# Finer first loads and the whole first batch of V turned on chip, in a chunked attention followed by a feed-forward block

## The chip, the cores and the metric

One core of a Trainium2 chip runs the whole kernel as one program. The metric is the device time of one execution in microseconds; the number compared is the median of several runs.

## The reference, cut to what matters

Batch 4, 8 heads, 768 tokens, head size 64, 8 memory tokens. Attention runs in chunks of 32 queries, each seeing the memory, 16 tokens to the left, its own 32 and 8 to the right; then each token's 512 numbers go through a normalisation and a two-layer block with 2048 hidden units.

```python
for c in range(nc):                       # chunks of 32 queries
    l_start, r_end = max(0, c_start - 16), min(S, c_end + 8)
    k_full = concat([mem_k, k[:, :, l_start:r_end]]); v_full = concat([mem_v, v[...]])
    a = softmax(scale * q_c @ k_full.T)
    out[:, :, c_start:c_end] = a @ v_full
x = out.transpose(0, 2, 1, 3).reshape(B, S, 512)
xn = (x - mean) / sqrt(var + 1e-6) * g_ln
return x + relu(xn @ w_ch1) @ w_ch2       # w_ch1 512x2048, w_ch2 2048x512
```

## The kernel before, in words

**Tiles and pairs.** The 3072 tokens are 24 tiles of 128; tile `t` belongs to batch `t // 6`. Two tiles are a pair `u`, and the feed-forward block works on pairs: `up(u, s)` (L398), eight steps of eight matmuls into `upb[s % 2]` with a ReLU on ACT or DVE, and `down(u, part)` (L415), eight parts of four matmuls into `dnb`; the last part of a tile adds the residual on DVE (L426) and stores the tile from SyncE (L429).

**Attention of a tile.** `qk_products` (L279), 32 small matmuls of Q against K; `below_max` (L298), maximum and subtraction on DVE; `weights` (L306), the exponential on ACT; `pt` (L313), P turned on TensorE and copied out half by DVE, half by ACT; `val_products` (L328), P times V into `two`; `tokens` (L339), division and mean on DVE; `shift` (L352), mean subtracted on GpSimd ("P") or ACT ("A"); `root` (L368), the standard deviation, on ACT and GpSimd; `turn_x` (L380), the tokens turned and scaled.

**Layout.** An octet is 8 consecutive tokens of one head, one row of 512 numbers. K and Q are loaded as octets (`load_octets`, L111), turned by 16 small transposes for each head pair `j` (`turn`, L222), and copied into `KT` (with the memory's columns between, `to_stream`, L237, two copies) or `QD` (`to_rows`, L246, one copy). V is wanted with tokens on partitions in 12 groups of 64 queries, with 40 tokens of overlap; it is loaded so by `load_v_group` (L118), from rows of 128 bytes, and the doubled rows are copied by SyncE (`v_shared`, L155, `v_mem`, L159). For batch 0 most of V is turned instead: octets into `VT` (which is `KT[1]`), then `v_turn(g, engine)` (L261) turns group `g` back and copies it into `V[0]`.

**Order of the work.** It is written out by hand: all engines run their instructions in the order of the source. TensorE's fillers, `warm(n)` (L444), multiply zeros into `upb[1]`. PSUM for the turns comes from a list of banks in rotation (`slot`, L86). Loads go out on the GpSimd queue; outputs and SBUF-to-SBUF copies on SyncE. From the third pair on a plan puts the attention of pair `u + 1` between the steps of `up(u)` and `down(u - 1)` (L653 to L715).

**The first 75 us** (L471 to L651). First loads: mem_k, 72 octets of K, 64 of Q, four V groups; then W1 in four parts, 72 octets of V, W2 in four, the rest of K (24 octets, two loads of 24 rows) and of Q. Tiles 0 and 1 use V groups 0 to 3, loaded directly; `v_twice` (L468) copies their doubled rows. Pair 0's `up` starts when tiles 0 and 1 are turned (L562). In between stand scores 2 and 3, V's turn and groups 4 to 11, tiles 2 and 3. Pair 1's `up` holds the rest of Q; pair 0's `down` holds the rest of K and tiles 4 and 5 (L611 to L639); half of pair 1's `down` is then issued with the turn of batch 1's K.

## Time and profile before

| what | number |
|---|---|
| median of 3 runs | 259.06 us (258.75 to 259.46) |
| the profiled execution | 258.69 us, its span 257.0 us |
| TensorE (PE) busy | 241.1 us, 94% of the span, 3411 matmuls |
| DVE, ACT, POOL busy | 131.9, 120.1, 97.5 us |
| L403 `up` and L419 `down` matmuls | 100.1 and 97.1 us |
| L447 fillers | 51 matmuls, 15.2 us |
| loads on the GpSimd queue | 14.68 MB in 41600 packets |

The span is what the profiler saw from the first to the last instruction; the rest of the execution's time lies around it. Times in the views are microseconds from the start of the span. A line of a timeline gives start, length, engine, source line, operation, what is written and read, a count, and in brackets the idle time before it and what ended it. PEld is TensorE's loading of weights, POOL is GpSimd, SPq the issuing of transfers by SyncE. The granted clock is the share of TensorE's clock that the chip lets through, in tenths in the page's slices.

### The profile page before, as it was taken

The numbers are of one execution on the slowest core, as the hardware profiler recorded it, in microseconds if no ns is written. First come the engines' busy times: TensorE is split into PE (matmuls) and PEld (weight loads), VectorE is DVE, ScalarE is ACT, GpSimd is POOL, SyncE is SP. The second block draws the span as 40 slices with busy tenths as digits, with TensorE's granted clock in tenths as the row PEclk, the third lists the DMA queues.
The fourth block names the chain that finished last, engine by engine and source line by source line (L and its number), as shares of the span: only waits on it lengthen the run. The fifth ranks groups of instructions, "written<-read, shape, count | busy, mean of one in ns | idle before, by whom it ended". The sixth has DMA issues, their size and how long they took to land.

```text
span 257.0 us, 7795 instructions
## 1 busy us (share of the span) xinstructions
PE 241.1 (94%) x3411; PEld 167.0 (65%) x3411; DVE 131.9 (51%) x296; ACT 120.1 (47%) x231; POOL 97.5 (38%) x171
## 2 busy tenths in 40 slices
PE   8697987997999899999999999999999999999993
PEld 3364675874577667667677767676677777777751
DVE  5557656345855656356555555554643564541121
ACT  1243466435565554654554455456464544543300
POOL 8397210372993286732402739512113022120000
PEclk9968999999999999999999999999999999999999
DMA  4999997099999997853398469805200111011112
GB/s 54 154 111 202 212 206 136 3 140 148 131 111 130 191 124 81 53 70 95 48 169 160 61 43 99 91 5 126 54 11 34 43 43 41 3 45 41 41 41 83
DMA packets 46462, 23.35 MB, mean 91 GB/s; under 512 B 33308, under 2 KB 42724, under 8 KB 46380
## 3 DMA queue, kind: packets, MB, share of 16 engines
q0 software_dynamic: 41600, 14.68, 50.0%
q1 hardware_dynamic: 4828, 8.18, 11.0%
q8 instruction: 26, 0.43, 0.7%
q14 instruction: 8, 0.07, 0.1%
HBM read 29.33 MB, written 6.29 MB: 139 GB/s over the span
## 4 chain that ended last, share of the span: by engine, by line
PE 76%; DMA 10%; DVE 5%; ACT 3%; POOL 2%; issue 1%; SPq 1%; DVEq 0%; ACTq 0%; POOLq 0%
PE upb L403 31%; PE dnb L419 31%; DMA raw<-in_q_dram 4%; PE two L332 3%; PE one L228 3%; DMA w1c<-in_moe_w_ch_dram 3%; DMA V<-memv 3%; PE one L290 2%; PE one L384 2%; PE one L317 1%; DVE KT L241 1%; ACT xn L359 1%; DVE xs L342 1%; ACT PTz L326 1%; POOL raw L113 1%
## 5 line engine op out<-in xcount | busy, mean ns | idle before, releaser
L403 PE MATMUL upb<-xT,w1c 128*128 128x256 f16 x768 | 100.1, 274 | 1.6 <-DVE xT L390 1.6
L419 PE MATMUL dnb<-w2c,rT 128*128 128x512 f16 x384 | 97.1, 380 | 0.0
L403 PEld LDWEIGHTS <-w1c 128*128 128x128 f16 x768 | 80.0, 115 | 10.2 <-issue 1.1
L411 ACT ACTIVATE rT<-upb 128x512 f16<-128x512 f32 x90 | 53.4, 593 | 60.4 <-PE upb L403 60.1
L419 PEld LDWEIGHTS <-rT 128*128 128x128 f16 x384 | 35.0, 98 | 26.7
L355 POOL TENSOR_SCALAR xn<-xs,nmean 128x512 f16<-128x512 f32 x18 | 12.4, 691 | 77.2 <-DVE nmean L348 44.3
L426 DVE SCALAR_TENSOR_TENSOR xs<-dnb,rstd,xs 128x512 f32<-128x512 f32 x24 | 18.0, 750 | 30.4 <-PE dnb L419 29.8
L307 ACT ACTIVATE P<-sub 128x512 f16<-128x512 f32 x24 | 15.2, 632 | 30.9 <-DVE sub L301 30.9
L390 DVE TENSOR_TENSOR xT<-one,g_col 128x512 f16<-128x512 f16 x22 | 15.2, 690 | 24.4 <-PE one L384 23.1
L228 PEld LDWEIGHTS <-raw 96*64 96x64 f16 (+2 forms) x640 | 14.6, 114 | 9.6 <-issue 6.0
L374 POOL TENSOR_SCALAR veps<-ssq 128x1 f32<-128x1 f32 x24 | 4.5, 189 | 40.2 <-ACT sq L370 39.9
L300 DVE TENSOR_REDUCE nmx<-one 128x8 f32<-128x512 f32 x22 | 15.1, 685 | 6.4 <-PE one L290 6.4
L370 ACT ACTIVATE sq<-xs,nmean 128x512 f16<-128x512 f32 x24 | 17.2, 717 | 0.3
L341 DVE RECIPROCAL rec<-two 128x8 f32<-128x8 f32 x24 | 5.0, 207 | 23.6 <-PE two L332 23.2
L342 DVE CUSTOM_DVE_ANT_1 xs<-two,rec 128x512 f32<-128x512 f32 x24 | 16.6, 691 | 0.8
L332 PEld LDWEIGHTS <-PTz 128*64 128x64 f16 x384 | 8.4, 110 | 12.3 <-issue 8.2
L447 PE MATMUL upb<-zeros 128*128 128x512 f16 x51 | 15.2, 437 | 1.3 <-DVE zeros L471 1.3
L332 PE MATMUL two<-V,PTz 128*64 128x65 f16 x384 | 11.0, 198 | 5.3 <-DVE V L469 1.7
L301 DVE TENSOR_TENSOR sub<-one,nmx 128x512 f32<-128x512 f32 x22 | 15.2, 691 | 0.8
L228 PE MATMUL one<-identity,raw 96*64 96x96 f16 (+2 forms) x432 | 13.4, 206 | 1.4 <-DMA raw<-in_q_dram 1.4
L378 POOL TENSOR_TENSOR rstd<-veps,mhalf 128x1 f32<-128x1 f32 x24 | 13.3, 554 | 2.0
L135 POOL DMA_DIRECT2D V<-in_v_dram x16 | 13.7, 856 | 0.4 <-issue 0.4
(107 smaller groups left out, 224.3 us busy)
## 6 DMA issues: line engine op xcount, KB each, us to landing
out_dram<-xs SPq DMA_DIRECT2D x24, 256.0 KB, 2.7
raw<-in_k_dram POOLq DMA_DIRECT2D x3, 768.0 KB, 8.6
raw<-in_q_dram POOLq DMA_DIRECT2D x3, 768.0 KB, 12.5
w1c<-in_moe_w_ch_dram POOLq DMA_DIRECT2D x4, 512.0 KB, 10.2
w2c<-in_moe_w_ch_dram POOLq DMA_DIRECT2D x4, 512.0 KB, 13.7
V<-in_v_dram POOLq DMA_DIRECT2D x16, 77.0 KB, 3.2
V<-in_v_dram POOLq DMA_DIRECT2D x15, 56.0 KB, 3.9
V<-memv SPq DMA_DIRECT2D x6, 120.0 KB
```

Of the source, the lines that this page charges most:

```text
L228: nc.tensor.matmul(out=pv[64 * par : 64 * par + 64, n * r : n * r + n], lhsT=src[lo : lo + n, heads + par, r, :], rhs=identity[lo : lo + n ...
L301: nc.vector.tensor_tensor(out=s.rearrange("p (c k) -> p c k", c=8), in0=scores, in1=free(m, 0, [[1, 8], [0, 64]]), op=ALU.subtract,)
L307: nc.scalar.activation(out=P[t % 3], in_=sub[t % 2], func=ACTF.Exp, scale=0.125)
L332: nc.tensor.matmul(out=two[64 * gg : 64 * gg + 64, 128 * h : 128 * h + 65], lhsT=PTz[t % 3][:, 4 * (h // 2) + 2 * gg + h % 2, :, :], rhs=V ...
L342: nc.vector.tensor_tensor_reduce(out=x.rearrange("p (h d) -> p h d", h=H), in0=free(two, 0, [[128, 8], [1, 64]]), in1=free(r, 0, [[1, 8], ...
L370: nc.scalar.activation(out=sq, in_=xs[t % 9], func=ACTF.Square, bias=nmean[t % 6], scale=1.0, accum_out=ssq[i],)
L390: nc.vector.tensor_tensor(out=xT[(t // 2) % 3][:, :, 128 * i : 128 * i + 128], in0=pv.rearrange("p (d c) -> p d c", d=4), in1=free(g_col, ...
L403: nc.tensor.matmul(out=p[:, 256 * hb : 256 * hb + 256], lhsT=free(w1c[hc // 4][:, dt, :], hc % 4, [[4, 128]]), rhs=xT[u % 3][:, dt, :], st ...
L411: nc.scalar.activation(out=o, in_=i, func=ACTF.Relu)
L419: nc.tensor.matmul(out=p, lhsT=rT[u % 2][:, hc, 128 * i : 128 * i + 128], rhs=w2c[hc // 4][:, hc % 4, :], start=(hc == 0), stop=(hc == 15),)
L426: nc.vector.scalar_tensor_tensor(out=x, in0=p, scalar=rstd[t % 9], in1=x, op0=ALU.mult, op1=ALU.add,)
L447: nc.tensor.matmul(out=upb[1], lhsT=zeros[:, 0:128], rhs=zeros, start=True, stop=True,)
```

## The change

- K, Q and V of batch 0 are first loaded as 64 octets each. The other 32 octets of each come as 128 rows (head pair by octet) in two loads, one for each head of the pair, into `rest[i]`.
- W1 comes in two loads of 1024 columns; W2's four follow at once. The order on the queue is K, Q, V, rest of K, half W1, rest of V, half W1, rest of Q, W2, mem_v.
- The direct loads of V groups 0 to 3, `v_twice` and the SyncE copy of mem_v for them go; V is turned for all twelve groups, the first four before pair 0's `up`. The turn of mem_v and V's first part stand between the scores of tiles 0 and 1 and their values.
- Fillers: 39 instead of 51.
- Scores 3 move into pair 0's `up`, as do the rest of K and `pt(2)`; tiles 4 and 5 are scored in pair 1's `up`. The loads of batch 1 are issued earlier. Pair 1's `down` is no longer begun before the third pair; all eight parts lie in the loop.
- `shift` of tiles 2 and 3 is on GpSimd instead of ACT.

```diff
-    def load_rest(dst, src, lo, n):
-        for hg in range(2):
+    def load_rest(i, src):
+        for par in range(2):
             nc.gpsimd.dma_start(
-                out=dst[32 * hg : 32 * hg + n, :, :, :],
-                in_=dram(src, 4 * hg * HS + 512 * lo, [[512, n], [HS, 4], [1, 512]]),
+                out=rest[i][:, par, :, :],
+                in_=dram(src, par * HS + 512 * 64, [[2 * HS, 4], [512, 32], [1, 512]]),
             )
...
-    load_octets(0, k, 0, 0, 72, 0)
+    load_octets(0, k, 0, 0, 64, 0)
     load_octets(1, q, 0, 0, 64, 0)
-    load_mem_rows(0, 1)
     make_identity(nc, identity)
-    for g in range(4):
-        load_v_group(0, g)
+    load_mem(memv0, mem_v, H)
+    load_octets(2, v, 0, 0, 64, 0)
...
+    load_rest(0, k)
+    load_w1(0)
+    load_rest(2, v)
+    load_w1(1)
+    load_rest(1, q)
+    for c in range(4):
+        load_w2(c)
+    load_mem_rows(0, B)
+    ready_v(1, nc.gpsimd)
...
-    warm(7)
+    warm(4)
     for j in range(4):
         turn_k_first(j, "VA"[j % 2])
     for j in range(4):
         turn_q_first(j, 0, "AV"[j % 2])
-    warm(2)
     s0 = qk_products(0)
     s1 = qk_products(1)
     below_max(0, s0)
...
     turn_q_first(3, 32, "A")
+    warm(1)
+    pt(0)
     weights(1)
+    mem_turn(memVT, memv0, H)
+    mem_cols(VT, memVT, False)
+    turn_v_first(0, "A")
+    turn_v_first(1, "V")
+    turn_v_first(2, "A")
+    turn_v_first(3, "V")
+    warm(1)
+    pt(1)
+    v_turn(0, "V")
+    v_turn(1, "A")
+    nc.vector.memset(V[0][96:128, NG - 1, :, :], 0.0)
+    warm(3)
+    val_products(0)
+    v_turn(2, "V")
+    v_turn(3, "A")
+    tokens(0)
+    shift(0, "A")
     warm(2)
+    val_products(1)
     s2 = qk_products(2)
+    warm(2)
+    tokens(1)
+    shift(1, "A")
+    warm(2)
+    turn_x(0)
+    turn_k_rest(0, "A")
+    warm(2)
+    turn_x(1)
+    warm(2)
+    up(0, 0)
     below_max(2, s2)
     weights(2)
+    turn_k_rest(1, "V")
+    up(0, 1)
+    turn_k_rest(2, "A")
+    turn_k_rest(3, "V")
+    up(0, 2)
+    v_turn(4, "V")
+    s3 = qk_products(3)
+    below_max(3, s3)
+    weights(3)
+    up(0, 3)
+    pt(2)
+    v_turn(5, "A")
+    turn_v_rest(0, "A")
+    turn_v_rest(1, "V")
+    val(2, "P")
...
+    up(1, 0)
     s4 = qk_products(4)
     below_max(4, s4)
     weights(4)
+    up(1, 1)
+    v_turn(9, "V")
+    up(1, 2)
     s5 = qk_products(5)
     below_max(5, s5)
     weights(5)
+    up(1, 3)
+    root(1)
+    v_turn(10, "V")
+    up(1, 4)
+    pt(4)
     root(2)
+    up(1, 5, "V")
+    v_turn(11, "A")
     root(3)
...
+    up(1, 6)
     pt(5)
     val(4, "A")
+    up(1, 7, "V")
+    banks["list"] = one + upb
+    down(0, 0)
...
-        d = 5 if u == 2 else 0
+        d = 4 if u == 2 else 0
...
-            elif u > 2:
+            else:
                 down(u - 1, step // 2)
-            elif step % 4 == 3:
-                down(u - 1, 4 + step // 4)
```

More of the change, by code (lines that the diff above doesn't have):

```diff
@@ L54 @@
     last = sb.tile([128, 1], FP16, name="last")
-    w1c = [sb.tile([128, 4, 512], FP16, name=f"w1c{i}") for i in range(4)]
+    w1c = [sb.tile([128, 4, 1024], FP16, name=f"w1c{i}") for i in range(2)]
     w2c = [sb.tile([128, 4, 512], FP16, name=f"w2c{i}") for i in range(4)]
@@ L60 @@
     QD = [sb.tile([128, 4, S], FP16, name=f"QD{i}") for i in range(2)]
-    krest = sb.tile([64, 4, 8, 64], FP16, name="krest")
-    qrest = sb.tile([64, 4, 8, 64], FP16, name="qrest")
+    rest = [sb.tile([128, 2, 8, 64], FP16, name=f"rest{i}") for i in range(3)]
     sub = [sb.tile([128, 512], FP32, name=f"sub{i}") for i in range(2)]
@@ L169, in load_w1 @@
         nc.gpsimd.dma_start(
-            out=w1c[c], in_=dram(moe_w_ch1, 512 * c, [[FF, 128], [128 * FF, 4], [1, 512]])
+            out=w1c[c], in_=dram(moe_w_ch1, 1024 * c, [[FF, 128], [128 * FF, 4], [1, 1024]])
         )
@@ L404, in up @@
                     out=p[:, 256 * hb : 256 * hb + 256],
-                    lhsT=free(w1c[hc // 4][:, dt, :], hc % 4, [[4, 128]]),
+                    lhsT=free(w1c[hc // 8][:, dt, :], 512 * (hc // 4 % 2) + hc % 4, [[4, 128]]),
                     rhs=xT[u % 3][:, dt, :],
@@ L451, in turn_k_first @@
     def turn_k_first(j, engine):
-        to_stream(KT[0], turn(raw[0], 2 * j, 0, 72), j, engine, 72, 0)
+        to_stream(KT[0], turn(raw[0], 2 * j, 0, 64), j, engine, 64, 0)
     def turn_k_rest(j, engine):
-        pv = turn(krest, 2 * (j % 2), 32 * (j // 2), 24)
-        to_stream(KT[0], pv, j, engine, 24, 72)
+        to_stream(KT[0], turn(rest[0], 0, 32 * j, 32), j, engine, 32, 64)
     def turn_q_first(j, lo, engine):
@@ L461, in turn_q_rest, with turn_v_first, turn_v_rest @@
     def turn_q_rest(j, engine):
-        pv = turn(qrest, 2 * (j % 2), 32 * (j // 2), 32)
-        to_rows(0, pv, j, engine, 32, 64)
-    def turn_v(j, engine):
-        to_stream(VT, turn(raw[2], 2 * j, 0, 72), j, engine, 72, 24)
-    def v_twice(g0, g1):
-        nc.vector.tensor_copy(out=V[0][32:64, g0:g1, :, :], in_=V[0][64:96, g0:g1, :, :])
+        to_rows(0, turn(rest[1], 0, 32 * j, 32), j, engine, 32, 64)
+    def turn_v_first(j, engine):
+        to_stream(VT, turn(raw[2], 2 * j, 0, 64), j, engine, 64, 0)
+    def turn_v_rest(j, engine):
+        to_stream(VT, turn(rest[2], 0, 32 * j, 32), j, engine, 32, 64)
     nc.vector.memset(zeros, 0.0)
@@ L484 @@
     )
-    nc.vector.memset(memv16[:, :, :, 64:VW], 1.0)
-    nc.vector.memset(V[0][:, 0:4, :, 64:VW], 1.0)
-    nc.vector.memset(V[0][0:16, 0, :, :], 0.0)
+    load_rest(0, k)
[7 more added lines that the diff above has]
+    ready_v(1, nc.gpsimd)
+    nc.vector.memset(VT[:, :, 0:16], 0.0)
+    nc.vector.memset(VT[:, :, KC - 8 : KC], 0.0)
     for i in range(3):
@@ L491 @@
     nc.vector.memset(mhalf, -0.5)
-    nc.vector.memset(VT[:, :, KC - 8 : KC], 0.0)
-    load_w1(0)
-    load_w1(1)
-    load_octets(2, v, 0, 24, 96, 0)
-    load_mem(memv0, mem_v, H)
-    load_w1(2)
-    load_w1(3)
-    load_w2(0)
-    load_w2(1)
-    ready_v(1, nc.gpsimd)
-    load_rest(krest, k, 72, 24)
-    load_rest(qrest, q, 64, 32)
-    load_w2(2)
-    load_w2(3)
-    load_mem_rows(1, B)
-    v_mem(0, (64,), 4)
+    nc.vector.memset(V[0][:, :, :, 64:VW], 1.0)
+    nc.vector.memset(V[0][0:16, 0, :, :], 0.0)
+    nc.vector.memset(memv16[:, :, :, 64:VW], 1.0)
     five = one + dnb + [upb[0]]
@@ L513 @@
     mem_cols(KT[0], memKT[:, 0:4, :], True)
-    nc.vector.memset(V[0][:, 4:NG, :, 64:VW], 1.0)
-    warm(7)
+    warm(4)
     for j in range(4):
@@ L529 @@
     turn_q_first(3, 32, "A")
+    warm(1)
+    pt(0)
     weights(1)
+    mem_turn(memVT, memv0, H)
[15 more added lines that the diff above has]
+    shift(0, "A")
     warm(2)
+    val_products(1)
     s2 = qk_products(2)
-    pt(0)
+    warm(2)
[6 more added lines that the diff above has]
+    turn_x(1)
+    four = one + dnb
+    banks["list"] = four
+    warm(2)
+    up(0, 0)
     below_max(2, s2)
     weights(2)
-    warm(4)
-    pt(1)
-    nc.vector.memset(V[0][96:128, NG - 1, :, :], 0.0)
+    turn_k_rest(1, "V")
[13 more added lines that the diff above has]
+    val(2, "P")
+    turn_v_rest(2, "A")
+    turn_v_rest(3, "V")
+    up(0, 4)
+    pt(3)
+    v_turn(6, "V")
+    v_turn(7, "A")
+    up(0, 5)
+    turn_x(2)
+    val(3, "P")
+    load_octets(0, k, 1, 0, 96, 0)
+    load_octets(1, q, 1, 0, 96, 0)
+    load_v_group(1, 0)
+    up(0, 6, "V")
+    turn_q_rest(0, "A")
+    turn_q_rest(1, "V")
     nc.vector.tensor_copy(
@@ L542 @@
     )
-    warm(6)
-    v_twice(0, 2)
-    val_products(0)
-    tokens(0)
-    shift(0, "A")
-    v_twice(2, 4)
-    warm(2)
-    pt(2)
-    val_products(1)
-    tokens(1)
-    shift(1, "A")
-    warm(2)
-    turn_x(0)
-    warm(4)
-    turn_x(1)
-    s3 = qk_products(3)
-    warm(2)
-    four = one + dnb
-    banks["list"] = four
-    up(0, 0)
-    below_max(3, s3)
-    up(0, 1)
-    weights(3)
-    mem_turn(memVT, memv0, H)
-    mem_cols(VT, memVT, False)
-    up(0, 2)
-    up(0, 3, "V")
-    turn_v(0, "A")
-    turn_v(1, "V")
-    turn_v(2, "A")
-    turn_v(3, "V")
-    pt(3)
-    up(0, 4)
-    v_turn(4, "V")
-    v_turn(5, "A")
-    val(2, "A")
-    up(0, 5)
-    v_turn(6, "V")
-    v_turn(7, "A")
-    up(0, 6)
-    val(3, "A")
-    turn_x(2)
-    up(0, 7, "V")
-    v_turn(8, "A")
-    turn_x(3)
-    root(0)
-    up(1, 0)
-    v_turn(9, "V")
-    up(1, 1, "V")
-    v_turn(10, "A")
-    up(1, 2)
-    root(1)
-    up(1, 3, "V")
-    v_turn(11, "V")
-    load_octets(0, k, 1, 0, 96, 0)
-    load_octets(1, q, 1, 0, 96, 0)
-    for g in range(3):
-        load_v_group(1, g)
-    up(1, 4)
-    up(1, 5, "V")
-    turn_q_rest(0, "A")
-    turn_q_rest(1, "V")
-    up(1, 6)
+    up(0, 7)
+    v_turn(8, "V")
+    turn_x(3)
     turn_q_rest(2, "A")
     turn_q_rest(3, "V")
-    up(1, 7, "V")
-    turn_k_rest(0, "A")
-    turn_k_rest(1, "V")
-    banks["list"] = one + upb
-    down(0, 0)
-    turn_k_rest(2, "A")
-    turn_k_rest(3, "V")
-    down(0, 1)
+    root(0)
+    load_v_group(1, 1)
+    up(1, 0)
     s4 = qk_products(4)
@@ L618 @@
     weights(4)
-    down(0, 2)
+    up(1, 1)
+    v_turn(9, "V")
+    up(1, 2)
     s5 = qk_products(5)
@@ L622 @@
     weights(5)
+    up(1, 3)
[3 more added lines that the diff above has]
+    pt(4)
     root(2)
+    up(1, 5, "V")
+    v_turn(11, "A")
     root(3)
-    for g in range(3, 8):
+    for g in range(2, 5):
         load_v_group(1, g)
-    down(0, 3)
-    down(0, 4)
-    pt(4)
-    down(0, 5)
+    up(1, 6)
     pt(5)
     val(4, "A")
+    up(1, 7, "V")
+    banks["list"] = one + upb
+    down(0, 0)
+    down(0, 1)
+    val(5, "A")
+    down(0, 2)
+    turn_x(4)
+    mem_cols(KT[1], memKT[:, 4:8, :], True)
+    down(0, 3)
+    root(4)
+    for g in range(5, 9):
+        load_v_group(1, g)
+    down(0, 4)
+    turn_x(5)
+    root(5)
+    for g in range(9, NG):
+        load_v_group(1, g)
+    down(0, 5)
+    turn_k(1, 0, "V")
     down(0, 6)
+    turn_k(1, 1, "A")
+    turn_k(1, 2, "V")
     down(0, 7)
-    val(5, "A")
-    root(4)
-    root(5)
-    for g in range(8, NG):
-        load_v_group(1, g)
-    mem_cols(KT[1], memKT[:, 4:8, :], True)
-    down(1, 0)
-    turn_k(1, 0, "V")
-    turn_x(4)
-    down(1, 1)
-    turn_k(1, 1, "A")
-    down(1, 2)
-    turn_k(1, 2, "V")
-    turn_x(5)
-    down(1, 3)
     turn_k(1, 3, "A")
```

## The prediction

> **What bounds the kernel now.** I read the summary page first, then the busy time by stage, the chain of waits, and the instruction timelines of each engine up to 100 us. The page's slices:

> ```profile
> PE   8697987997999899999999999999999999999993
> ...
> PEclk9968999999999999999999999999999999999999
> ```

> TensorE is the bound: it is busy in nearly every slice after the eighth, and each slice is 6.4 us. The busy time by stage (columns: stretch, its length, busy us of PE, PEld, DVE, ACT and POOL, granted clock, DMA share, GB/s) says how much of it is not work:

> ```profile
> 0.00:29.44 29.44, 23.28 (x439) 13.21 (x440) 17.69 (x47) 9.48 (x19) 19.83 (x36) 0.88 1.06 140
> 29.44:100.00 70.56, 64.89 (x1082) 47.04 (x1081) 40.09 (x92) 37.42 (x76) 33.77 (x58) 1.00 0.94 130
> 100.00:245.00 145.00, 145.00 (x1858) 103.34 (x1857) 71.83 (x156) 72.57 (x135) 43.91 (x78) 1.00 0.41 64
> ```

> From 100 us on PE never idles, and the change touches nothing that is issued there. So the end moves by two things only: when the first `up` of the first pair starts (29.44 us, call it T0), and how much PE idles between T0 and 100 us (70.56 - 64.89 = 5.67 us). All 51 filler matmuls of `warm` (L447) lie before T0, so taking twelve away saves nothing by itself. The waits behind the 5.67 us (who waited for whom, us, times, longest):

> ```profile
> PE upb L403 <- DVE xT L390: 1.6, 2, 0.8
> PE two L332 <- ACT PTz L326: 1.5, 2, 1.3
> PE two L332 <- ACT V L273: 1.1, 2, 0.9
> PE two L332 <- DMA V<-memv: 0.6, 1, 0.6
> ```

> What sets T0 is a chain, read from the PE timeline (start, length):

> ```profile
> 12.66 0.42 PE L228 MATMUL one<-identity,raw 32*64 32x32 f16 x16 [1.39 <-DMA raw<-in_q_dram]
> ...
> 14.38 0.87 PE L290 MATMUL one<-KT,QD 64*32 64x64 f16 x50
> ...
> 28.26 0.40 PE L384 MATMUL one<-identity,xn 128*128 128x128 f16 x4 [0.35 <-ACT xn L359]
> ```

> Q lands at 12.62; the first scores start 1.76 us later; then softmax, P turned, values, tokens, x turned, 15.06 us in all. The last view is the granted clock in stretches of 3.41 us, at whose edges it changed:

> ```profile
> 10.78:14.19 3.41, 2.02 (x98) 1.58 (x90) 2.03 (x6) 2.05 (x6) 1.38 (x4) 1.00 1.46 108
> 14.19:17.60 3.41, 3.00 (x125) 2.56 (x126) 2.53 (x5) 0.91 (x3) 3.29 (x8) 0.50 0.90 84
> 17.60:21.02 3.42, 3.42 (x54) 1.63 (x50) 1.25 (x3) 1.97 (x5) 3.42 (x5) 0.50 1.24 202
> 21.02:24.43 3.41, 2.66 (x30) 1.44 (x29) 2.48 (x8) 1.25 (x3) 3.24 (x6) 1.00 1.24 201
> ```

> The same stretches for L447 alone hold 0.41, 0.26, 2.33 and 2.22 us of filler. After the one with 0.41 the clock fell to half; 3.00 busy us of small turns and scores did not bring it back, 2.33 us of filler did; 1.66 and 1.78 us in two other stretches kept it.

> **Part 1: the loads.** The first K, 72 octets, is issued at 2.03 and lands at 10.00, Q at 12.62. After, both have 64 octets: 64 KB less before Q is complete. At the 162 GB/s of the stretch from 5 to 8 us that is 0.4 us: Q at 12.2. The other end comes from the later K and Q of batch 1 (96 rows each, 1536 KB, 196 GB/s from 54 to 57 us): issued at 50.85, the second landed at 62.76, 11.9 us; with the 2.7 us of the small mem_k load as the fixed part, (11.9 - 2.7) x 1024/1536 + 2.7 = 8.8, so Q at 10.9. The second is nearer in kind, a K and a Q back to back in the same queue, so I lean there: **11.2**.

> [...]

> The queue behind: POOL's loads wait for the landing of the one eight loads earlier (the first fetch of qrest waited 3.07 us for raw V, the load eight before it). In the new order none starves the queue: 2.9 MB lie ahead of the end of the first W1 half, at about 0.2 MB/us from 4 us on, so it lands near 20, the second half near 27, long before T0 and the fifth `up`. V's rest (near 22) and the 1.0-1.5 us memsets of `ready_v` (done near 26) are covered as well. The four direct V groups with their SyncE copies and `v_twice` go; with them the 0.97 and 0.75 us PE waits on L469.

> **Part 2: from the first scores to T0.** Times from the start of the first scores. P0 is ready at 3.6 (14.38 to 17.96, unchanged: ACT still copies Q first). Then `pt` of tile 0 (0.6 at half clock), DVE 0.42, ACT 0.58: 5.5. ACT now has exp 1 (0.63) and two V turns (0.70 for 72 octets, so 0.65 each): 7.45; DVE's two V turns, 0.75 each behind the mem copies (0.19 + 0.26), end at 7.65. Only then can `v_turn` 0 and 1 start: 8.7; ACT copies the second (0.57) behind P1's half (0.58): 9.3. `warm(3)` ends at 9.85 at half clock (0.43 each), value products 10.4, `v_turn` 2 and its DVE copy 11.15, which stands on DVE ahead of `tokens(0)`; that takes 0.21 + 0.69 + 0.08 + 0.15 and issue: 12.35. Value products 1, scores 2 and `warm(4)` in two calls follow, `tokens(1)` 13.95, the ACT shift 14.7, x turned twice with `turn_k_rest(0)` and two fillers between, DVE 0.69: T0 at **18.0** if the clock stays at half to the end. With PE's rows at their full-clock length (a filler 0.22, `pt` 0.39, a turn 0.30 against 0.47) from the first score on, the same list gives 13.3; with full-clock lengths only after 24.4 us, 16.0; only after 27.8 us, 17.1.

> Which? The new order has hardly a filler from 8.3 us to the first value products, so the drop at 14.19 stays. The stretch to 17.6 and the next hold one or two fillers (0.4 to 0.9 us), that to 24.4 `warm(3)` (1.3 us), that to 27.8 six (2.6 us). Only the last passes the 2.33 that was seen to suffice: clock back at 27.8, T0 = 11.2 + 1.76 + 17.1 = **30.1**, 0.7 us later than now. So V's turn, which adds about 4 us of ACT and DVE work in the chain, eats the earlier Q and the fillers that go.

> [...]

> **Part 3: from T0 to 100 us.** PE work: out go `mem_turn` of V (0.34), four turns of 72 octets (33.49 to 34.73: 1.24) and one K rest (0.30); in come scores 3 (0.34), `pt(2)` (0.24) and four turns of V's rest (two of Q's rest took 0.61, so 1.2): -0.1 us. No filler lies here. The waits, scheduled by hand on four engines with `up` 0.97 (PE), ReLU 0.60, exp 0.63, max and subtract 0.69 each, root 0.90, PTz 0.42 (DVE) and 0.58 (ACT):
> - pair 0: DVE does two softmaxes before `val(2)`; exp 3 cannot start until 6.0 after T0, and ReLU 3, ACT's half of PTz 2 and V 5 stand behind it on ACT: 8.45. PE is there at 6.85: **1.6** (now 1.16 + 0.23 in the same place). xT 3 before pair 1: **0.2** (now 0.50 + 0.78).
> - pair 1: exp 4 and 5 wait for DVE with ReLUs behind them, and roots 1 to 3 (2.7 us) come in the same ten microseconds: **0.2** on `upb`. Then `down(0, 0)` writes dnb0, where `pt(5)` was put; ACT's copy of it stands behind root 2, V 11, root 3 and a ReLU and ends at 29.9, PE is there at 28.5: **1.4** (now 1.30 at the value products).
> - pair 2: its `down` is now full, so V's mem rows (issued by SyncE after the outputs of `down(0, 7)`, about 8 us as now) have 11.8 us of PE work before value products 6: no wait where now 0.62; the rest (now 1.07) **0.4**, as a `down` lies between the last values and the turn.

> Sum 3.8 against 5.67, -1.9. The batch 1 loads start some 10 us earlier; V groups on POOL end later than root 5 by 11 us, but tile 6 needs only the first four. If that cover goes, the 0.62 comes back.

> **Sum.** The profiled execution took 258.69 (span 257.0 and 1.7 around it): 258.69 + 0.7 - 0.1 - 1.9 = 257.4. It lay 0.37 under the median of the runs, 259.06, so on that scale **257.8**.

> **Rivals.**
> - *The clock stays up.* For it: small matmuls are busy time too, and 0.97 us of filler before 10.78 may suffice. Against: 14.19 to 17.60. T0 = 13.0 + 13.3 = 26.3: -3.1 - 0.1 - 1.9, **253.9**.
> - *Slower: the clock is still at half when `up` begins.* Place: the stretch up to 27.8 with six fillers spread between waits. For it: a stretch just under 2.33. T0 31.2 with 0.2 for Q's turns at half, +1.8; one more stretch of 3.41 us of `up` at half loses 1.7: +1.8 + 1.7 - 0.1 - 1.9 = +1.5, **260.6**. It decides once T0 and the loss on the `up`s together pass 29.44 + 2.0 + 0.8 = 32.2.
> - *The waits only move.* ACT is 53% and DVE 57% busy now from T0 to 100 us, but by the list above ACT has 9.3 us of work in 11.3 us of pair 1; if each in-order wait costs a little more, 5.7 us idle stays: +0.7 - 0.1 = +0.6, **259.7**, no measurable change.

> **Chances.** Forecast 0.45 (256.6 to 259.0, which covers Q at 10.9 to 12.2 and the clock back at 24.4), clock up 0.20, clock down 0.20, waits move 0.15. A measurement of this kernel tells about 0.3% (0.8 us) from no change. Faster: 0.33 of the forecast's and 0.20: 0.53. Same: 0.10 and 0.10: 0.20. Slower: 0.02, 0.05, 0.20: 0.27. The range reaches to both outer rivals: 254.0 to 260.7.

> **What would show it.** Right: Q landing near 11.2; granted clock 0.50 from about 14 to 28; T0 near 30; a PE wait of 1 to 2 us on ACT before value products 2 and before `down(0, 0)`; no wait on V's mem rows; PE idle from T0 to 100 us near 3.8. Wrong: a clock back before 22 (time near 254), T0 past 32, a PE wait on W1 or V's rest, or idle time above 5.7 after T0.

## The result and the profile after

| | before | after |
|---|---|---|
| median of 4 runs each, same chip | 258.9 us (258.68 to 259.46) | 261.72 us (261.12 to 262.48) |
| ratio, 95% interval | | 1.0107 (1.007 to 1.0144) |
| the profiled execution, its span | 258.69, 257.0 us | 261.19, 259.5 us |
| Q's landing | 12.62 | 10.14 |
| first scores | 14.38 | 11.83 |
| T0, the first `up` of pair 0 | 29.44 | 32.88 |
| granted clock at half | 14.19 to 21.02 | 13.26 to 26.91 |
| PE idle in the 70.56 us after T0 | 5.67 | 4.41 |

The change costs 2.8 us, 1.1%, and the time lies outside the predicted range. The table says where: Q comes 2.5 us earlier, the waits after T0 shrink by 1.3, and yet T0 is 3.4 us later. Line numbers of the changed kernel are one lower than before's (L402 for L403); an experiment with a line added has its own.

The summary page of after: TensorE's busy share in slices of 6.5 us, the granted clock, and the queue that brings instructions (packets, MB, share).

```profile
PE   8948897998999989999999999999999999999992
...
PEclk9955999999999999999999999999999999999999
...
q8 instruction: 27, 0.44, 0.7%
```

The third slice (13.0 to 19.5 us) has fallen to 4 where before had 9. The busy time by stage shows that the rest of the kernel is as it was:

```profile
32.88:103.44 70.56, 66.15 (x1124) 48.35 (x1125) 41.54 (x96) 38.67 (x78) 35.34 (x59) 1.00 0.81 108
103.44:248.44 145.00, 145.00 (x1827) 102.97 (x1826) 70.76 (x152) 72.02 (x135) 42.24 (x75) 1.00 0.40 62
```

Idle after T0 is 70.56 - 66.15 = 4.41 us, and PE is still full in the last stretch. So the loss is ahead of T0. PE's timeline there:

```profile
11.83 1.09 PE L289 MATMUL one<-KT,QD 64*32 64x64 f16 x55
16.53 0.31 PE L289 MATMUL one<-KT,QD 64*32 64x64 f16 x9 [3.60 <-issue]
...
20.94 0.24 PE L227 MATMUL one<-identity,raw 64*64 64x64 f16 x2
22.45 1.01 PE L227 MATMUL one<-identity,raw 64*64 64x64 f16 x30 [1.28 <-issue]
...
32.88 1.04 PE L402 MATMUL upb<-xT,w1c 128*128 128x256 f16 x8 [0.44 <-DVE xT L389]
```

This is the finding. PE stops in the middle of a group of equal matmuls: after 55 of the 64 scores of tiles 0 and 1, and after 2 of the 16 matmuls that turn V's third head pair into one bank (the timeline merges them with those of the fourth). Their inputs are there: K and Q of both tiles come from the same turns and copies as those of the scores that ran, and V is one load into one tile. The profile names no semaphore and writes "issue". Number PE's recorded instructions from 0, matmuls, weight loads and the two of other kinds at the start together: the first stop is before number 449 and the second before number 705, 256 later. Before has the first at the same number, though another program leads up to it; its T0 is the second line:

```profile
15.66 0.39 PE L290 MATMUL one<-KT,QD 64*32 64x64 f16 x14 [0.41 <-issue]
...
29.44 1.91 PE L403 MATMUL upb<-xT,w1c 128*128 128x256 f16 x16
```

| block from | PE enters the block before | packet starts to ends | the last instruction started in the block before ends | PE enters |
|---|---|---|---|---|
| before, 449 | 10.88 | 13.28 to 14.17 | 15.26 | 15.66 |
| before, 705 | 15.66 | 19.44 to 20.34 | 22.05 | 22.10 |
| after, 449 | 10.41 | 13.75 to 15.11 | 12.82 | **16.53** |
| after, 705 | 16.53 | 20.12 to 21.17 | 21.09 | **22.45** |

In these four rows the packet starts 2.4 to 3.8 us after PE has entered the block before, takes 0.9 to 1.4 us, and when PE is waiting its code runs 1.3 to 1.5 us after the packet's end (first, third and fourth row; 1.4 to 1.5 at 449 in the three experiments below whose packet times are given). In after PE needed only 2.4 us (10.41 to 12.82) for a block of small matmuls. The transfers of 10 to 24 us (busy share of the DMA engines in 40 slices; packets by queue):

```profile
DMA  9999999999999999999999999999999999999999
...
q0 software_dynamic: 3411, 2.75, 117.5%
q8 instruction: 2, 0.03, 1.1%
```

Two instruction packets stand among 3411 data packets, with the DMA engines busy 90% or more in every slice. The two stops cost PE 3.60 + 1.28 = 4.88 us. (These waits count from the end of the last matmul, 12.92 and 21.18, a little later than the ends in the table.)

### The profile page after: what moved, and what is told of

Same layout as the page of the kernel before. It is cut to its first block, busy times and chain, and to the rows that moved or that the text cites. A ratio compares the mean times of both kernels' runs of the same rounds, so it can differ in the third digit from the quotient of the medians.

```text
span 259.5 us, 7955 instructions
## 1 busy us (share of the span) xinstructions
PE 242.7 (94%) x3495; PEld 169.5 (65%) x3495; DVE 131.2 (51%) x298; ACT 121.7 (47%) x237; POOL 93.5 (36%) x164
## 4 chain that ended last, share of the span: by engine, by line
PE 90%; DVE 3%; issue 3%; ACT 2%; DVEq 0%; ACTq 0%
PE upb L402 33%; PE dnb L418 33%; PE one L227 5%; PE upb L446 5%; PE two L331 3%; PE one L289 3%; PE one L383 2%; PE one L316 2%; PE dnb L227 1%; PE upb L227 1%; DVE xT L389 1%; PE one L267 1%; ACT rT L410 1%; DVE sub L300 1%; DVE nmx L299 1%
## 5 line engine op out<-in xcount | busy, mean ns | idle before, releaser
L402 PE MATMUL upb<-xT,w1c 128*128 128x256 f16 x768 | 100.9, 274 | 2.1 <-DVE xT L389 1.9
L402 PEld LDWEIGHTS <-w1c 128*128 128x128 f16 x768 | 79.6, 115 | 10.9 <-issue 1.6
L410 ACT ACTIVATE rT<-upb 128x512 f16<-128x512 f32 x93 | 55.1, 593 | 59.9 <-PE upb L402 59.7
L418 PEld LDWEIGHTS <-rT 128*128 128x128 f16 x384 | 35.3, 98 | 27.8 <-issue 1.3
L354 POOL TENSOR_SCALAR xn<-xs,nmean 128x512 f16<-128x512 f32 x20 | 13.9, 695 | 97.7 <-DVE nmean L347 50.3
L227 PEld LDWEIGHTS <-raw 96*64 96x64 f16 (+2 forms) x640 | 15.3, 118 | 8.2 <-issue 8.0
L299 DVE TENSOR_REDUCE nmx<-one 128x8 f32<-128x512 f32 x21 | 14.4, 687 | 9.8 <-PE one L289 9.8
L227 PE MATMUL one<-identity,raw 96*64 96x96 f16 (+2 forms) x432 | 14.0, 209 | 1.3 <-issue 1.3
L289 PEld LDWEIGHTS <-QD 64*32 64x32 f16 x768 | 7.3, 93 | 11.9 <-issue 11.3
L300 DVE TENSOR_TENSOR sub<-one,nmx 128x512 f32<-128x512 f32 x21 | 14.5, 691 | 0.7
L446 PE MATMUL upb<-zeros 128*128 128x512 f16 x39 | 13.6, 490 | 1.3 <-DVE zeros L468 1.3
L240 DVE COPY KT<-one 128x192 f16<-128x192 f16 (+4 forms) x24 | 10.9, 495 | 6.5 <-PE one L227 5.0
L377 POOL TENSOR_TENSOR rstd<-veps,mhalf 128x1 f32<-128x1 f32 x24 | 13.3, 556 | 2.0
## 6 DMA issues: line engine op xcount, KB each, us to landing
w2c<-in_moe_w_ch_dram POOLq DMA_DIRECT2D x4, 512.0 KB, 16.8
```

The costliest lines, as they stand in the source:

```text
L227: nc.tensor.matmul(out=pv[64 * par : 64 * par + 64, n * r : n * r + n], lhsT=src[lo : lo + n, heads + par, r, :], rhs=identity[lo : lo + n ...
L299: nc.vector.tensor_reduce(out=m, in_=scores, axis=AX.X, op=ALU.max)
L300: nc.vector.tensor_tensor(out=s.rearrange("p (c k) -> p c k", c=8), in0=scores, in1=free(m, 0, [[1, 8], [0, 64]]), op=ALU.subtract,)
L402: nc.tensor.matmul(out=p[:, 256 * hb : 256 * hb + 256], lhsT=free(w1c[hc // 8][:, dt, :], 512 * (hc // 4 % 2) + hc % 4, [[4, 128]]), rhs=x ...
L410: nc.scalar.activation(out=o, in_=i, func=ACTF.Relu)
L418: nc.tensor.matmul(out=p, lhsT=rT[u % 2][:, hc, 128 * i : 128 * i + 128], rhs=w2c[hc // 4][:, hc % 4, :], start=(hc == 0), stop=(hc == 15),)
```

## The theories

- **A, the code.** PE's next 256 instructions wait behind the data loads that the new order puts on the queue early (V, the rests, W1), and PE has less work between the two edges to cover it. Hold the loads back and the wait goes; the place is tied to the instruction's number.
- **B, the chain.** V's turn, now in front of the first values, and the engines it occupies make T0 late; "issue" is a label for something that belongs to these instructions.
- **C, the fillers.** Twelve fillers fewer leave the clock at half for longer, and that is the time lost.

## The experiments

All times are against before on the same chip, whose median was 259.03 to 259.06 in the three groups. "Gaps", or code waits, are the two waits at instructions 449 and 705.

### All later loads held back until Q is turned

```diff
-    load_mem(memv0, mem_v, H)
-    load_octets(2, v, 0, 0, 64, 0)
...
-    ready_v(1, nc.gpsimd)
...
         turn_q_first(j, 0, "AV"[j % 2])
+    nc.gpsimd.tensor_copy(out=gate, in_=QD[0][:, 3, 0:1])
+    load_mem(memv0, mem_v, H)
+    load_octets(2, v, 0, 0, 64, 0)
+    load_rest(0, k)
...
+    ready_v(1, nc.gpsimd)
```

The copy into `gate` makes GpSimd wait for Q's last turned columns before it issues the loads.

> The changed kernel, with every load after the first K and Q issued only when Q's first 32 octets have been turned. Theory A (code): PE stands still at its 449th and 705th instruction because the next 16 KB of its program is fetched only when it enters the 16 KB before, and that fetch waits behind the data loads. Then the first gap (3.60 us now) falls below 0.8, the second (1.28 now) becomes 1 to 3 as W1 is in flight, T0 comes to 29.5 to 31 and the time to 258.5 to 260. Theory B (chain): the gaps belong to the work there (a bank, a copy) and T0 is late through V's turn and the half clock. Then the gaps stay, V lands 4 us later, T0 is 33 or later, time 261.5 or more.

Measured: 259.82 us (257.92 to 261.43, 10 runs), ratio 1.0033 (0.9996 to 1.007); T0 30.40. PE's waits from 10 to 33 us:

```profile
PE dnb L228 <- DMA raw<-in_v_dram: 2.0, 1, 2.0
PE two L332 <- DVE xsum L342: 0.7, 1, 0.7
PE one L290 <- issue: 0.5, 1, 0.5
```

The 3.60 is 0.52 and the 1.28 is gone, with not one PE instruction changed. (For the second I had expected 1 to 3 us.) The packet for block 449 now runs from 11.42 to 12.38, against 13.75 to 15.11. A new wait of 1.95 us for V, which lands at 19.21 instead of 13.44, takes part of it back.

### V after Q's turn, everything else after V's turn

```diff
         turn_q_first(j, 0, "AV"[j % 2])
+    nc.gpsimd.tensor_copy(out=gate[:, 0:1], in_=QD[0][:, 3, 0:1])
+    load_mem(memv0, mem_v, H)
+    load_octets(2, v, 0, 0, 64, 0)
...
     turn_v_first(3, "V")
+    nc.gpsimd.tensor_copy(out=gate[:, 1:2], in_=VT[:, 3, 16:17])
+    load_rest(0, k)
...
+    ready_v(1, nc.gpsimd)
```

> As before it, but V's first part alone is issued after Q's turn, and everything after that (rests, W1, W2) only when V's first part has been turned, some 16 us after the start. Theory A: both gaps fall below 0.8 us, T0 comes to 28 to 29.5, time 257 to 258.5. Theory B: the gaps stay, T0 33 or later, time 261.5 or more.

Measured: 267.29 us (266.79 to 267.98), ratio 1.0318 (1.0291 to 1.0345). The gaps are 0.72 and none, as A has it, but the kernel is far slower:

```profile
34.90 1.47 PE L403 MATMUL upb<-xT,w1c 128*128 128x256 f16 x6 [4.16 <-DMA w1c<-in_moe_w_ch_dram]
```

W1 lands at 34.86, PE stands for it, and the clock falls to half twice more (34.5 to 41.35 and 48.2 to 51.6). The gain that I expected is missed: holding loads back has a price as soon as one of them is needed at T0.

### 120 more PE instructions of no more work

```diff
-        for _ in range(n):
+        w = 512 // parts
+        for _ in range(n * parts):
             nc.tensor.matmul(
-                out=upb[1], lhsT=zeros[:, 0:128], rhs=zeros, start=True, stop=True,
+                out=upb[1][:, 0:w], lhsT=zeros[:, 0:128], rhs=zeros[:, 0:w], start=True, stop=True,
             )
...
-    warm(20)
+    warm(20, 4)
```

> The changed kernel with each of the first 20 fillers cut into four of 128 columns: the same PE time before the first K, 120 more PE instructions. Theory A: the gaps stay at the same instruction numbers, so they move 120 instructions forward in the program, the first to before the first scores, with about 2 us each; T0 is 1 to 2.5 us earlier, time 259 to 260.7. Theory B: the gap stays inside the scores of tile 1 with 3.6 us; T0 and time (261 to 262.5) unchanged.

Measured: 261.67 us (260.88 to 262.36), ratio 1.0098 (1.0069 to 1.0127).

```profile
13.95 0.29 PE L227 MATMUL upb<-identity,raw 32*64 32x32 f16 x5 [2.01 <-issue]
...
20.43 0.29 PE L227 MATMUL one<-identity,raw 32*64 32x32 f16 x5 [3.08 <-issue]
```

Both stops have left the scores and V's turn and stand in turns of Q, which are other instructions and again numbers 449 and 705. So the place belongs to the count; B's reading of "issue" falls. A's price is missed: 5.09 us instead of 4.88, T0 33.30 instead of 32.88, no gain. Moving the blocks' edges did not help here.

### Before, with its first K as 64 octets and 8

```diff
-    load_octets(0, k, 0, 0, 72, 0)
+    load_octets(0, k, 0, 0, 64, 0)
+    load_octets(0, k, 0, 64, 72, 64)
```

> The kernel before with one edit: the first K as 64 octets and, right behind, the other 8 in a small load of their own. Both theories: K and Q land earlier, Q near 10.5 instead of 12.6. Theory A: the program's block at instruction 449 is not there before about 15, so T0 is at most 0.7 us earlier, time 258.2 to 259. Theory B: the chain simply starts 2 us earlier, T0 27.5, time 256.5 to 257.2.

Measured: 257.36 us (257.1 to 257.51), ratio 0.9932 (0.9912 to 0.9951). Q lands at 11.25 instead of 12.62, T0 is 28.08 instead of 29.44, and the clock is at half only from 16.30 to 19.71. The wait at 449 grows as A says, but A's time, 258.2 to 259, is missed: I had the code there at about 15, and its packet ran from 12.02 to 13.13 (13.28 to 14.17 in before), so PE went on at 14.6. Why it started 1.2 us after PE entered the block before, and not 2.4 as in before, was not tried. The wait costs less than Q brings:

```profile
14.61 0.29 PE L290 MATMUL one<-KT,QD 64*32 64x64 f16 x14 [1.06 <-issue]
```

### V issued when K is turned, the rest when Q is turned

```diff
         turn_k_first(j, "VA"[j % 2])
+    nc.gpsimd.tensor_copy(out=gate[:, 0:1], in_=KT[0][:, 0, 16:17])
+    load_mem(memv0, mem_v, H)
+    load_octets(2, v, 0, 0, 64, 0)
     for j in range(4):
         turn_q_first(j, 0, "AV"[j % 2])
+    nc.gpsimd.tensor_copy(out=gate[:, 1:2], in_=QD[0][:, 3, 0:1])
+    load_rest(0, k)
...
+    ready_v(1, nc.gpsimd)
```

The loads' old places are empty, as above.

> The changed kernel, V's first part issued when the first of K's turns is copied (about 10.4 us, just after PE enters the block whose start sends for the code at 449), all other loads when Q has been turned. Theory A (code): the fetch for 449 finds the queue nearly empty, so that gap is below 0.8 us; V lands near 16, so the 1.95 us that PE waited for V in the version with everything held back goes too; the fetch for 705 is behind V and the rests and costs 0 to 1.5. T0 28 to 29.5, profiled time 256.5 to 258. Theory B (chain and clock): V or the gap costs the same as in the version held back, T0 30 to 31, 258.5 to 260.

Measured: 257.37 us (255.85 to 258.62, 9 runs), ratio 0.9929 (0.9903 to 0.9955); T0 29.04.

```profile
11.78 1.09 PE L290 MATMUL one<-KT,QD 64*32 64x64 f16 x55
13.53 0.31 PE L290 MATMUL one<-KT,QD 64*32 64x64 f16 x9 [0.66 <-issue]
...
18.36 1.01 PE L228 MATMUL one<-identity,raw 64*64 64x64 f16 x30 [0.17 <-issue]
...
29.04 1.04 PE L403 MATMUL upb<-xT,w1c 128*128 128x256 f16 x8 [0.44 <-DVE xT L390]
```

The gaps fall from 4.88 to 0.83 us, V (16.71) is in time, and T0 comes 3.84 us earlier: the change's own PE program, with the loads in another order, is 0.7% faster than before instead of 1.1% slower. Packet 449 starts 0.5 us after PE has entered the block before (10.36, then 10.85 to 12.07), not 3.3.

### After, with the twelve fillers back

```diff
-    warm(4)
+    warm(7)
...
+    warm(2)
     s0 = qk_products(0)
...
-    warm(1)
+    warm(3)
     pt(0)
...
-    warm(1)
+    warm(3)
     pt(1)
...
-    warm(3)
+    warm(6)
     val_products(0)
```

> The changed kernel with twelve fillers put back before the first values (51 in all): 7 before K's turn, 2 before the first scores, 3 and 3 before the two turns of P, 6 before the first values. Theory A: the gaps at 449 and 705 stay, the fillers only add; T0 32.5 to 34, time 261 to 262.8. Rival C (the fillers that went are the cost, by the half clock): the clock is back one or two stretches of 3.41 us earlier, T0 31 to 32, time 259.5 to 260.8.

Measured: 263.26 us (262.83 to 264.78), ratio 1.0169 (1.0121 to 1.0216); T0 34.80, gaps 3.53 and 0.50, clock at half from 14.96 to 28.61: four stretches of 3.41 us, as in after. T0 and time lie above even A's ranges, and far from C's. The fillers cost time and raise no clock earlier. C falls.

### `pt(5)` in another PSUM bank

```diff
+    banks["turn"] += 2
     pt(5)
+    banks["turn"] -= 2
```

> The changed kernel with the turn of P of tile 5 in another PSUM bank, so that the first part of pair 0's down need not wait for it. All theories: the wait of 1.08 us before that part goes and nothing takes its place, as the waits after T0 are apart from what happens before: 0.8 to 1.1 us less than the changed kernel, 260.6 to 261.0.

Measured: 260.2 us (258.9 to 261.04, 10 runs), ratio 1.0035 (1.001 to 1.006). In after PE's waits from 32 to 105 us hold

```profile
PE two L331 <- ACT PTz L325: 1.3, 1, 1.3
PE dnb L418 <- ACT PTz L325: 1.1, 1, 1.1
```

and here the second line is gone; idle after T0 goes from 4.41 to 3.34. T0 is also 0.83 us earlier, with gaps of 3.12 and 1.27, although nothing ahead of it was touched; so the 1.5 us between the medians of the two versions, more than the 0.8 to 1.1 expected, are not the bank's alone.

### Both edits together

V issued when K is turned, the rest when Q is turned, and `pt(5)` in the other bank; of the two diffs:

```diff
+    nc.gpsimd.tensor_copy(out=gate[:, 0:1], in_=KT[0][:, 0, 16:17])
...
+    nc.gpsimd.tensor_copy(out=gate[:, 1:2], in_=QD[0][:, 3, 0:1])
...
+    banks["turn"] += 2
     pt(5)
+    banks["turn"] -= 2
```

> Both of these edits, the order of the loads and the bank. Theory A: the gains add, T0 28 to 29.5, profiled time 255.5 to 257. Theory B: 257.5 to 259.

Measured: 255.02 us (254.53 to 255.34), ratio 0.9834 (0.9805 to 0.9863). No wait at 449 or 705 is left, T0 is 27.91, idle after it 3.34; T0 and time are a little better than expected. This version beats both kernels, by 1.7% of before.

### Exponential 3 issued after tile 2's values

On top of both edits:

```diff
     below_max(3, s3)
-    weights(3)
...
     val(2, "P")
+    weights(3)
```

> The version with the loads held back and the other bank, and one edit more: the exponential of tile 3 on ACT is issued after the values of tile 2, so that the ReLU of pair 0's step 3, ACT's half of tile 2's P and group 5 of V no longer stand behind it. If the wait of 1.29 + 0.39 us before the values of tile 2 comes from that order on ACT, as the prediction put it, it falls to 0.6 to 1.0 and the time from 255.0 to 254.0 to 254.6. If it comes from DVE's half of P or from V's turn on PE, it stays and so does the time.

Measured: 255.22 us (254.47 to 257.98, 6 runs), ratio 0.9861 (0.9823 to 0.9898). The wait for ACT's half of PTz 2 shrinks as foreseen:

```profile
PE two L332 <- ACT PTz L326: 0.4, 1, 0.4
PE two L332 <- ACT V L273: 0.4, 1, 0.4
```

It was 1.3; idle after T0 is 2.45 instead of 3.34. So ACT's order caused it. The median is no better than that of the version before it: the 0.9 us do not show in runs that spread by 3.5.

### Before with the 64 octets and its loads held back

```diff
-    load_octets(0, k, 0, 0, 72, 0)
+    load_octets(0, k, 0, 0, 64, 0)
+    load_octets(0, k, 0, 64, 72, 64)
...
         turn_k_first(j, "VA"[j % 2])
+    nc.gpsimd.tensor_copy(out=gate[:, 0:1], in_=KT[0][:, 0, 16:17])
+    load_mem_rows(0, 1)
+    for g in range(4):
+        load_v_group(0, g)
...
         turn_q_first(j, 0, "AV"[j % 2])
+    nc.gpsimd.tensor_copy(out=gate[:, 1:2], in_=QD[0][:, 3, 0:1])
+    load_w1(0)
...
+    v_mem(0, (64,), 4)
```

> The kernel before with K as 64 and 8 octets, and its loads held back in the same way: mem_v and V groups 0 to 3 until K's first turn is copied, the rest until Q is turned. Theory A (code): the gap of 1.06 us at instruction 449 that the split of K alone left falls below 0.4; the small V packets come later, which may cost some of it at the first values. T0 27.2 to 28.2, time 256.3 to 257.4. If holding the loads back helps by something else than the code fetch, the gap stays.

Measured: 258.05 us (256.55 to 258.69, 11 runs), ratio 0.9954 (0.9933 to 0.9975). The code wait at 449 is gone, but the direct V groups now land at 13.6 to 18.1 and PE waits for their doubled rows:

```profile
21.65 0.44 PE L333 MATMUL two<-V,PTz 128*64 128x65 f16 x16 [1.32 <-DVE V L470]
24.29 0.44 PE L333 MATMUL two<-V,PTz 128*64 128x65 f16 x16 [1.44 <-DVE V L470]
```

They were 0.88 and 0.98 us without the hold. T0 is 27.90 against 28.08, and the median is 0.7 us above the one without the hold; I expected a gain. Its profiled execution is 0.16 us faster instead, so why the medians lie so far apart stays open.

## Why the prediction was wrong, point by point

**The step that failed** is Part 2, "T0 = 11.2 + 1.76 + 17.1 = 30.1". Its list has a duration for every instruction of four engines and takes for granted that PE's instructions are there. The 17.1 us from first scores to T0 became 21.05 (11.83 to 32.88), and 4.88 us of code wait lie inside. In the version with V issued early, where 0.83 us of it are left, the same distance is 29.04 - 11.78 = 17.26, and its 257.37 stands beside the forecast 257.8. That closeness is partly luck: the clock there came back at 23.39, not at 27.8. For a clock back at 24.4 the same list gave 16.0; with 0.83 of code wait that is 16.8, still within 0.5 us of the 17.26. In before the distance is 15.06, so what the forecast said of V's turn, that it eats the earlier Q, agrees with the runs once the code is there: this version and before with its K split end at the same 257.4.

The sum on the profiled executions, against the predicted 257.4 and the measured 261.19:

| term | predicted | measured | difference |
|---|---|---|---|
| start of the first scores (Q 11.2 + 1.76) | 12.96 | 11.83 | -1.13 |
| first scores to T0 | 17.1 | 21.05 | +3.95 |
| idle after T0 | 3.8 | 4.41 | +0.6 |
| other time after T0, against before | -0.1 | +0.3 | +0.4 |

The differences add up to 3.8 us. "Other" is the span less T0 and idle: 222.2 against 221.9. The page puts `up`'s matmuls at 100.9 us in after and 100.1 before; what made them longer was not tried.

**Part 1, the loads: right in direction, too small.** Q at 11.2 was taken from a later load, with 10.9 as the earlier end; it was 10.14. From issue to landing the first K took 7.97 us with 72 rows and 5.24 with 64, 0.66 of the time for 0.89 of the rows. In before with its K split the same 64 rows took 6.0 us, 0.75 of the 7.97. Why the time fell by more than the rows was not tried. "In the new order none starves the queue" was true for data (W1's halves landed at 21.46 and 27.20) and left out the code, whose packets for 449 and 705 started 3.3 and 3.6 us after PE had entered the blocks before.

**The clock: nearly right.** Half from 14.19 to 27.8 was forecast, four stretches; it was 13.26 to 26.91, four stretches. In the predicted columns, for after:

```profile
13.26:16.67 3.41, 0.14 (x9) 0.14 (x8) 1.01 (x2) 0.00 (x0) 1.26 (x2) 0.50 1.17 209
16.67:20.09 3.42, 3.42 (x96) 2.88 (x88) 1.80 (x3) 1.81 (x5) 0.56 (x1) 0.50 1.18 192
20.09:23.50 3.41, 2.13 (x67) 1.99 (x66) 1.21 (x4) 2.28 (x6) 1.75 (x3) 0.50 1.15 209
23.50:26.91 3.41, 3.41 (x30) 1.66 (x31) 1.92 (x5) 1.39 (x3) 2.96 (x5) 0.50 1.19 198
```

In the first PE is busy for 0.14 us: the code wait also empties a stretch. With V issued early and that wait nearly gone, the clock fell as soon (13.15) but came back after three stretches (23.39). In the second PE is busy throughout, with only 0.61 us of filler among small turns, and the clock stayed at half. The fourth holds 1.97 us of filler, and the clock came back after it, so the 2.33 that I had taken as what suffices was not the least after which it came back.

**Part 3, the waits after T0: right in place, two of them too small.** Value products 2: 1.29 + 0.39, forecast 1.6. `down(0, 0)`: 1.08, forecast 1.4, and the bank as its cause is shown by the run with another bank. V's mem rows: gone, as forecast. Pair 1's turned x: 0.47, forecast 0.2. Pair 2's: 0.94 before the third pair, forecast 0.4. The 0.2 on `upb` in pair 1 does not show.

**The rivals.** The clock did not stay up. The slower rival's mechanism, a clock still at half when `up` begins, did not happen either; T0 passed its point of decision, 32.2, for another reason. Nor did the waits only move: idle after T0 fell to 4.41. That code can be late was in none of them, though the 0.41 us "issue" at 15.66 stood in the trace of before, in the midst of 64 equal matmuls.

**What is settled and what is not.** Shown: the place goes by the instruction's count; the wait goes when the queued loads go, with the same PE instructions; the fillers are not the cause. By which rule the DMA engines serve a code packet among data packets was not tried.

## What to carry to other kernels

An idle "issue" inside a run of equal instructions, at a distance of 256 from another, was late code here: where you meet one, look for the instruction packets among the data transfers. This start phase of many small matmuls uses up its code in 2.4 to 6.4 us a block (the four rows of the table of events), so do not queue there all the loads that one can: issue what is needed next, and hold the rest until the engine has its code, but no longer than its first use allows. When finer loads bring the first operand earlier, take that gain by itself first; here it was worth 0.7% without any of the rest.

## What was unexpected of the hardware

- In after, among queued loads, it took 6.1 us from PE's entering the block before 449 until the code at 449 ran (10.41 to 16.53); its packet of 16,384 bytes took 1.36 us of that. PE entered a later block at 42.65 us, and the next packet, the only one of any queue from 42 to 44 us, started 0.3 us later and took 0.95 us (42.91 to 43.86).
- The profiled executions met the 3.41 us stretches of the clock at different phases: the clock first rose at 3.95 us in before and at 6.43 in after. Runs of one kernel seem to differ by it. With all loads held back, the runs with a mean granted clock of 0.978 or 0.979 took 257.92 to 258.63 us, one at 0.973 took 258.75 and one at 0.972 took 259.39, those at 0.966 or 0.967 took 260.24 to 261.43; one more stretch at half is 0.5 x 3.41 / 260 = 0.0066 of the mean clock. A run at 0.956 took 261.34, no longer than those, so the clock is not the whole spread.
